# A fused gated-linear-attention and squared-ReLU kernel: the third and fifth unit's front steps, three hidden-layer steps and one output store take other places in the written order of the engines

## The chip, the cores and the metric

The kernel runs on 1 core of one Trainium2 chip. The metric is the device time of one execution in microseconds (us). The kernel before takes 170.76 us, the median of 3 runs (170.74 to 170.88).

## The reference

The program computes a recurrent linear attention with a decay for each channel, and puts its output through a two-layer network with a squared ReLU.

```python
def _attn_ref(q, k, v, alpha):               # each (4, 8, 768, 48), float32
    state = np.zeros((B, H, D, D))
    for t in range(S):
        state = alpha[:, :, t, :, None] * state + np.einsum('bhd,bhe->bhde', k[:, :, t], v[:, :, t])
        y[:, :, t] = np.einsum('bhd,bhde->bhe', q[:, :, t], state)
    return y

def _moe_ref(x, w_in, w_out):                # x (3072, 384), w_in (384, 2048), w_out (2048, 384)
    r = np.maximum(x @ w_in, 0.0)
    return (r * r) @ w_out
```

Here B = 4, H = 8, S = 768, D = 48; alpha lies between 0.8 and 1.0; x is y with its heads side by side.

## The kernel before

**Units.** The sequence of each batch is cut into 3 blocks of T = 256 tokens, which makes 12 units, numbered from 0: unit g is block g // 4 of batch g % 4. A partition holds two neighbouring tokens (j = 0, 1), so a unit fills the 128 partitions.

**The front of a unit** (from the third unit on, `decays_by_pair`). `pr` (L570) multiplies the two decays of a pair of tokens. `ln` (L573) takes the logarithm of that product into `lab`, `lm` (L612) the logarithm of the second decay alone into `la1` (shown as `la` by the profile). `m1i` (L579 and L582) sums `lab` over the tokens with a triangular matrix on TensorE, into PSUM bank `psW` (the first of `psWH`). `ei`, `ea`, `ec` (L590, L592, L595) take exponentials of the sums, `bk` (L597 on GpSimd, L599 on VectorE) multiplies one of them by a decay, `lb` (L614) subtracts `la1` from the sums, `es` (L616) takes the exponential of that. `ekm` (L646) and `eqm` (L641) multiply keys and queries by these factors into `qks`; `vc` (L637 on ScalarE) copies the values to bf16. Keys and queries are then transposed into `kqt`: for the units 0 to 2 on TensorE (`tr`, L669, with copies `et` out of PSUM, L677 and L679), from unit 3 on by two DMA transposes of SyncE's queue (`tr0`, `tr1`, L657).

**The mix.** `p` (L877, L730) forms the scores and the sum of key and value products, `mk` (L894) masks the scores (one half from `psZ`, one from `psX`), `y` (L765, L757) applies them and the state, `xe` and `xf` (L911, L913) copy the result to bf16, `xt` (L929 on TensorE for units 0 to 3, a DMA transpose L935 later) transposes it, and `xv` (L941, L943) copies the transposed result out of `psX` into `xt`, the input of the hidden layer. This last is the mix copy of the change's short name.

**The hidden layer.** For unit g and u = 0 to 7, `s1_g_u` (L992) makes two of 16 blocks of 128 hidden values for all 256 tokens, 6 matmuls into one PSUM bank; `re` (L1000 on ScalarE, L1002 on VectorE) is the ReLU out of that bank into a buffer `rr`; `sq` (L1010 on VectorE, L1013 on GpSimd, L1014 on ScalarE) squares one or two of them into `gt`. `s2_g_j_0` to `_3` (L1038) are the second layer for one token of each pair, four matmuls each; `oe` (L1045, L1047) copies the sum to `osb`, and `out` (L1054) stores it.

**Banks.** The hidden layer has two PSUM banks of `psWH` of its own, and for the first two units it also uses `psO`, in a fixed sequence (`HIDDEN = "0102102102102101"`, 2 meaning `psO`). So `s1_1_1` needs the bank that `re0_6` empties, `s1_1_4` the one that `re1_1` empties, `s1_1_5` the one that `re1_2` empties, and `s1_2_2` the one that `re2_0` empties. `rr` has 4 buffers of two halves; `re1_6` writes the half that `sq0_6` reads, `re1_7` the one that `sq0_7` reads.

**What sets the order.** `TABLES` (L206 to L268) names, for each of the five engines, every step in the sequence in which it is issued; an entry such as `+512` is a matmul on zeros at the start. `arrange` (L86) puts the steps in this order, `place` (L122) works out which semaphores each step must wait for, `emit` (L173) writes the programs. Each engine runs its list strictly in order: a step that waits holds everything behind it on its engine. A DMA is issued by the engine in whose list it stands.

Of the kernel before, what the change touches and what calls it, by code (L numbers as in the profile page):

```python
# [205 lines left out]
TABLES = {  # L206
    "act": """
        table ln0_0 ln1_0 ei0_0 xcaus ea0_0 ei1_0 ea1_0 ec1_0 et00_0 ec0_0 vc0 ln1 et01_0 et11_0 vc1 ei1 ea1 xe0
        ec1 et0_1 re0_0 sa1 re0_1 sq0_1 re0_3 xe1 re0_4 re0_5 lm2 ln2 re0_6 ei2 ea2 ec2 es2 re1_2 re1_3 sq0_6
        re1_4 et0_2 vc2 re1_6 sa2 sq1_6 sq1_3 ln3 lm3 ei3 ea3 ec3 es3 oe0_0 oe0_1 xf2 xe2 lm4 ln4 vc3 ei4 ea4  # L210
        ec4 re2_0 re2_1 es4 oe1_0 re2_2 re2_3 re2_4 ldk5 re2_5 ldq5 sa3 sq2_5 lm5 re2_7 ln5 re2_6 xe3 ei5 ea5
        ec5 xv3 es5 oe2_0 re3_0 oe2_1 lm6 re3_1 xe4 ln6 re3_4 re3_3 ei6 ea6 ec6 re3_6 sq3_5 re3_7 sq3_7 es6
        re4_0 re4_1 re4_2 re4_3 vc6 xe5 lm7 ln7 re4_7 oe3_1 re4_4 ei7 ea7 ec7 re4_6 sq4_6 es7 oe4_0 re5_0 re5_1
        lm8 ln8 xe6 re5_2 re5_3 ei8 ea8 re5_4 re5_5 es8 re5_6 re5_7 sq5_7 re6_0 re6_1 re6_2 oe5_0 vc8 xe7 lm9
        ln9 re6_5 re6_6 oe5_1 re6_7 ei9 ea9 es9 oe6_0 vc9 re7_0 lm10 re7_1 ln10 xe8 re7_3 ei10 ea10 re7_4 re7_5
        es10 re7_6 re7_7 oe7_0 re8_0 re8_1 re8_2 lm11 ln11 xe9 re8_3 re8_4 ei11 ea11 re8_5 re8_6 sq8_5 es11
        sq8_7 re9_0 oe8_0 vc11 re9_1 oe8_1 xe10 re9_3 re9_4 re9_5 re9_6 re9_7 re10_0 oe9_0 re10_1 re10_2 xe11
        oe9_1 re10_3 re10_4 re10_5 re10_6 re10_7 re11_0 oe10_0 re11_1 re11_2 re11_3 oe10_1 re11_4 re11_5 re11_6
        re11_7 oe11_0 oe11_10
    """,  # L220
    "dve": """
        zero zlinc zlstr zident zcaus zcaus1 zla0 zla1 zones zown zown0 zown1 zqk0 zqk1 zqk2 zlb0 zlb1 ekm0_0
        eqm0_0 ekm1_0 eqm1_0 et10_0 mk0_0 sa0 mk1_0 ekm1 eqm0_1 eqm1_1 xv0 et1_1 sc0 mk1_1 mk0_1 sc1 re0_2 xf1
        sq0_3 xv1 pr2 sq0_5 re0_7 re1_0 lb2 re1_1 ekm2 eqm0_2 eqm1_2 sq0_7 re1_5 et1_2 sq1_1 sq1_5 re1_7 mk1_2
        pr3 sc2 mk0_2 lb3 eqm1_3 eqm0_3 ekm3 xv2 pr4 sq1_7 bk4 lb4 ekm4 eqm1_4 eqm0_4 sq2_1 mk1_3 mk0_3 sc3
        oe1_1 sd3 sq2_7 sq2_6 xf3 lb5 ekm5 eqm1_5 eqm0_5 sa4 mk1_4 mk0_4 re3_2 pr6 sc4 sq3_1 xf4 sq3_3 re3_5
        sq3_6 lb6 ekm6 sa5 mk0_5 sc5 mk1_5 eqm0_6 eqm1_6 oe3_0 xf5 sq4_1 re4_5 pr7 sq4_3 sq4_7 sq4_5 bk7 lb7
        eqm0_7 sa6 eqm1_7 ekm7 sc6 sd6 mk0_6 mk1_6 pr8 oe4_1 xf6 sq5_3 bk8 lb8 ekm8 sq5_5 sq5_6 sa7 mk0_7 sc7
        mk1_7 eqm0_8 eqm1_8 sq6_1 re6_3 sd7 sq6_3 pr9 xf7 re6_4 sq6_5 sq6_6 sq6_7 bk9 lb9 ekm9 eqm0_9 eqm1_9
# [888 lines left out]
```

## Time and profile before

| | |
|---|---|
| median of 3 runs | 170.76 us |
| the profiled execution, its own time | 171.26 us |
| its span, first to last instruction | 169.5 us |
| TensorE (PE) busy | 163.8 us, 97% of the span |
| VectorE (DVE) busy | 118.0 us, 70% |
| ScalarE (ACT) busy | 109.6 us, 65% |
| GpSimd (POOL) busy | 35.3 us, 21% |
| DMA | 33.37 MB, mean 197 GB/s |
| granted TensorE clock | 1.0 throughout |

The profiled execution took 1.76 us more than its span and 0.50 us more than the median of the runs. A profile line gives the start in us from the span's start, the duration, the engine, the source line, the operation, the tile written and the tiles read, with the number of equal instructions in a row (x12); in brackets stands how long the engine stood idle before it, and who ended the idle time. PE is the matmul side of TensorE, PEld its loading of weights, SPq an issue of SyncE's DMA queue. Several matmuls overlap in the array, so that a row of twelve lasts some 0.16 us longer than the time until the next row can start.

### The profile page before, as it was taken

The numbers are of one execution on the slowest core, as the hardware profiler recorded it, in microseconds if no ns is written. First come the engines' busy times: TensorE is split into PE (matmuls) and PEld (weight loads), VectorE is DVE, ScalarE is ACT, GpSimd is POOL, SyncE is SP. The second block draws the span as 40 slices with busy tenths as digits, with TensorE's granted clock in tenths as the row PEclk, the third lists the DMA queues.
The fourth block names the chain that finished last, engine by engine and source line by source line (L and its number), as shares of the span: only waits on it lengthen the run. The fifth ranks groups of instructions, "written<-read, shape, count | busy, mean of one in ns | idle before, by whom it ended". The sixth has DMA issues, their size and how long they took to land.

```text
span 169.5 us, 5392 instructions
## 1 busy us (share of the span) xinstructions
PE 163.8 (97%) x2369; PEld 125.9 (74%) x2369; DVE 118.0 (70%) x206; ACT 109.6 (65%) x212; POOL 35.3 (21%) x46
## 2 busy tenths in 40 slices
PE   7988999999799999999999999999999999999994
PEld 2556889767686697877778876788797788787773
DVE  6577899985849868975978977887969637342130
ACT  3968778786868388667477757375677374466440
POOL 4671879130172032100240000000600000000000
DMA  5999999989999998999989999979797761040012
GB/s 137 324 318 188 260 312 215 293 288 252 185 220 329 241 181 197 307 137 243 301 195 247 263 152 258 207 194 288 145 190 205 97 119 58 0 141 4 33 60 93
DMA packets 68407, 33.37 MB, mean 197 GB/s; under 512 B 63520, under 2 KB 65312, under 8 KB 68384
## 3 DMA queue, kind: packets, MB, share of 16 engines
q1 hardware_dynamic: 62784, 24.39, 65.6%
q0 software_dynamic: 3520, 7.87, 18.6%
q10 hardware_dynamic: 2080, 0.79, 1.8%
q8 instruction: 18, 0.29, 0.7%
q14 instruction: 5, 0.04, 0.1%
HBM read 25.17 MB, written 4.72 MB: 176 GB/s over the span
## 4 chain that ended last, share of the span: by engine, by line
PE 83%; DMA 12%; ACT 1%; POOL 1%; issue 1%; DVE 0%; SPq 0%
PE psO L1038 34%; PE psWH L992 33%; DMA raw<-in_alpha_dram 6%; DMA raw<-in_v_dram 3%; DMA raw<-in_k_dram 2%; PE psX L877 2%; PE psZ L765 2%; PE psX L953 2%; PE psWH L1038 2%; PE psWH L730 1%; PE psZ L877 1%; PE psX L765 1%; PE psO L992 1%; PE psWH L579 1%; POOL raw L463 1%; ACT rr L1000 1%
## 5 line engine op out<-in xcount | busy, mean ns | idle before, releaser
L992 PE MATMUL psWH<-xt,win 128*128 128x256 bf16 x552 | 70.5, 273 | 0.9 <-ACT rr L1000 0.9
L1038 PE MATMUL psO<-wout,gt 128*128 128x384 bf16 x352 | 67.0, 326 | 0.0
L992 PEld LDWEIGHTS psWH<-xt,win 128*128 128x128 bf16 x552 | 59.8, 114 | 7.4 <-ACT rr L1000 1.4
L1000 ACT ACTIVATE rr<-psWH 128x512 bf16<-128x512 f32 x79 | 46.5, 599 | 25.3 <-PE psWH L992 24.0
L1038 PEld LDWEIGHTS psO<-wout,gt 128*128 128x128 bf16 x352 | 32.7, 98 | 16.7 <-DVE gt L1010 0.2
L1010 DVE TENSOR_TENSOR gt<-rr 128x1024 bf16<-128x1024 bf16 (+1 forms) x46 | 26.6, 584 | 22.4 <-ACT rr L1000 22.4
L1013 POOL TENSOR_TENSOR gt<-rr 128x1024 bf16<-128x1024 bf16 x3 | 5.7, 1911 | 56.6 <-ACT rr L1000 56.6
L894 DVE TENSOR_TENSOR pm<-psZ,caus 128x1024 bf16<-128x1024 f32 x12 | 14.6, 1216 | 3.7 <-PE psWH L730 3.0
L1045 ACT ACTIVATE osb<-psO 128x384 f32<-128x384 f32 x17 | 8.4, 492 | 11.6 <-PE psO L1038 11.2
L894 DVE TENSOR_TENSOR pm<-psX,caus 128x1024 bf16<-128x1024 f32 x12 | 14.6, 1215 | 0.9 <-PE psX L877 0.5
L641 DVE TENSOR_TENSOR qks<-raw,eq 128x384 bf16<-128x384 f32 x22 | 11.4, 550 | 1.1 <-ACT eq L616 1.0
L646 DVE TENSOR_TENSOR qks<-raw,ek 128x768 bf16<-128x768 f32 x11 | 10.5, 950 | 1.1 <-ACT ek L558 1.0
L1002 DVE TENSOR_SCALAR rr<-psWH 128x512 bf16<-128x512 f32 x13 | 8.8, 683 | 1.2 <-PE psWH L992 1.2
L1014 ACT ACTIVATE gt<-rr 128x512 bf16<-128x512 bf16 (+1 forms) x11 | 8.9, 821 | 0.6 <-DVE rr L1002 0.4
L573 ACT ACTIVATE lab<-prd 128x384 bf16<-128x384 f32 x10 | 5.2, 522 | 6.0 <-DVE prd L570 5.8
L1086 PE MATMUL psO<-zero 128*128 128x512 bf16 (+1 forms) x27 | 7.7, 418 | 1.3 <-DVE zero L382 1.3
L913 DVE CAST xbf<-psZ 128x384 bf16<-128x384 f32 x10 | 5.5, 554 | 3.4 <-PE psZ L757 3.2
L850 POOL TENSOR_TENSOR sbd<-tmp,acm 128x192 bf16<-128x192 f32 x5 | 2.9, 588 | 20.6 <-DVE tmp L840 16.2
L911 ACT ACTIVATE xbf<-psX 128x384 bf16<-128x384 f32 x11 | 5.4, 490 | 2.4 <-PE psZ L757 2.3
L637 ACT ACTIVATE vbf<-raw 128x768 bf16<-128x768 f32 x7 | 5.9, 837 | 1.2 <-DMA raw<-in_v_dram 1.2
L570 DVE TENSOR_TENSOR prd<-raw 128x384 f32<-128x384 f32 x9 | 6.4, 707 | 0.2 <-DMA raw<-in_alpha_dram 0.2
L616 ACT ACTIVATE eq<-la 128x384 f32<-128x384 f32 x10 | 5.2, 522 | 2.0 <-DVE la L614 2.0
(130 smaller groups left out, 190.8 us busy)
## 6 DMA issues: line engine op xcount, KB each, us to landing
out_dram<-osb SPq DMA_DIRECT2D x11, 384.0 KB, 3.3
raw<-in_alpha_dram SPq DMA_DIRECT2D x9, 384.0 KB, 5.5
raw<-in_v_dram SPq DMA_DIRECT2D x9, 384.0 KB, 4.4
raw<-in_k_dram SPq DMA_DIRECT2D x8, 384.0 KB, 5.7
raw<-in_q_dram SPq DMA_DIRECT2D x8, 384.0 KB, 4.0
win<-in_moe_w_in_dram POOLq DMA_DIRECT2D x4, 384.0 KB, 8.8
wout<-in_moe_w_out_dram POOLq DMA_DIRECT2D x4, 384.0 KB, 8.9
raw<-in_k_dram POOLq DMA_DIRECT2D x3, 384.0 KB, 6.4
```

Source lines behind the costliest of these rows:

```text
L570: add("dve", lambda e: e.tensor_tensor(hd(PRD[la][:]), al(0), al(1), ALU.mult), dve_ns(HD), p0, reads=[("raw", r, 0)], writes=[("prd", la) ...
L641: add("dve", lambda e, j=j, dst=dst: e.tensor_tensor(dst, RAW[r][:, 2, :, j, :].rearrange("p (n x) d -> p n x d", x=2), EQ[la][:, j].rearr ...
L646: add("dve", lambda e, a=a, E=E: e.tensor_tensor(QKS[qs][:, a, :, :, 0:D], RAW[r][:, 1 + a].rearrange("p h j d -> p j h d"), E[la][:].rear ...
L894: add("dve", lambda e, hf=hf, psT=psT: e.tensor_tensor(PM[pm][:, hf].rearrange("p r n j t -> p (r n) (j t)"), psT[:, :, :].rearrange("p r ...
L992: ins = pe.matmul(psN[:, i * T:(i + 1) * T], WIN[:, kk, hidden(fj)], mov, start=(kk == 0), stop=(kk == KT - 1))
L1000: add("act", lambda e, psN=psN, rr=rr: e.activation(rr, psN, AF.Relu), act_ns(512), pu + 600, reads=[keyN], writes=[("rr", rb, half)], nam ...
L1002: alts={"dve": (lambda e, psN=psN, rr=rr: e.tensor_scalar(rr, psN, 0.0, None, ALU.max), dve_ns(512))})
L1010: add("dve", lambda e, dst=dst, sq=sq: e.tensor_tensor(dst, sq, sq, ALU.mult), 148 + k * 267, pu + 1200, reads=[("rr", rb, h) for h in ran ...
L1014: "act": (lambda e, dst=dst, sq=sq: e.activation(dst, sq, AF.Square), act_ns(k * 512))})
L1038: ins = pe.matmul(psS, GT[gt][:, fj, j, :], WOUT[:, fj, :], start=(fj == 0), stop=(fj == FT - 1))
L1045: add("act", lambda e, j=j, psS=psS: e.activation(OSB[ob][:, j], psS, AF.Copy), act_ns(DM), ps_ + 700, reads=[keyS], writes=[("osb", ob, j ...
L1086: pr.arrange(TABLES, lambda n: lambda pe: pe.matmul(psO[:, 0:n], ZERO[:, 0:128], ZERO[:, 0:n], skip_group_check=True), zero)
```

## The change

Only `TABLES` changes: names move within the list of an engine, and one moves from ScalarE's to VectorE's. What is computed stays the same, and no step is added or removed.

```diff
     "act":
-        xe1 re0_4 re0_5 lm2 ln2 re0_6 ei2 ea2 ec2 es2 re1_2 re1_3 sq0_6 re1_4 et0_2 vc2 re1_6
+        xe1 re0_4 re0_5 re0_6 ln2 lm2 ei2 ea2 ec2 es2 re1_2 re1_3 vc2 re1_4 et0_2 re1_6
     "dve":
-        re0_7 re1_0 lb2 re1_1 ekm2 eqm0_2 eqm1_2 sq0_7 re1_5 et1_2 sq1_1 sq1_5 re1_7
+        re0_7 re1_0 re1_1 lb2 ekm2 eqm0_2 eqm1_2 re1_5 sq0_6 et1_2 sq0_7 sq1_1 sq1_5 re1_7
...
-        eqm0_3 ekm3 xv2 pr4 sq1_7 bk4 lb4
+        eqm0_3 ekm3 pr4 xv2 sq1_7 bk4 lb4
     "pe":
-        xt2 s2_1_0_2 s1_2_0 s1_2_1 m1i4 s2_1_0_3 s1_2_2 s1_2_3
+        xt2 s2_1_0_2 m1i4 s1_2_0 s1_2_1 s2_1_0_3 s1_2_2 s1_2_3
     "sp":
-        tr0_3 tr1_3 lda5 ldv4 tr0_4 tr1_4 out0_1 ldv5
+        tr0_3 tr1_3 lda5 out0_1 ldv4 tr0_4 tr1_4 ldv5
```

**First place, VectorE between the first and the second unit's hidden layer.** The `psO` row is the ReLU `re1_1`, the `rr2` row `re1_5`, the L614 row `lb2`, the L677 row the copy `et1_2` of the third unit's transposed keys and queries.

```order
 L1002 TENSOR_SCALAR rr0<-psWH 128x512
+L1002 TENSOR_SCALAR rr0<-psO 128x512
 L614 TENSOR_TENSOR la10<-psWH,la10 128x384
-L1002 TENSOR_SCALAR rr0<-psO 128x512
 L646 TENSOR_TENSOR qks2<-raw2,ek0 128x16x48
 L641 TENSOR_TENSOR qks2<-raw2,eq0 128x4x2x48 x2
+L1002 TENSOR_SCALAR rr2<-psWH 128x512
 L1010 TENSOR_TENSOR gt0<-rr3 128x512
-L1002 TENSOR_SCALAR rr2<-psWH 128x512
 L677 COPY kqt2<-psZ 128x8x2x64
+L1010 TENSOR_TENSOR gt0<-rr3 128x512
 L1010 TENSOR_TENSOR gt1<-rr0 128x1024
```

`re1_1` and `re1_5` stand one place sooner. The upper square was `sq0_7` and is now `sq0_6`, which came from ScalarE; `sq0_7` stands behind the copy `et1_2`, so that the list from there on has one square more ahead of it.

**Second place, TensorE and VectorE around the third unit's mix copy.** On TensorE the L579 and L582 rows are `m1i4`, the sums of the fifth unit's decays; `xt2` is what the mix copy fills.

```order
 L1038 MATMUL psO<-wout,gt1 128x384 x4
-L992 MATMUL psWH<-xt2,win 128x256 x12
 L579 MATMUL psWH<-lab0,linc 128x384
 L582 MATMUL psWH<-ones2,lab0 128x2 x4
+L992 MATMUL psWH<-xt2,win 128x256 x12
 L1038 MATMUL psO<-wout,gt1 128x384 x4
 L992 MATMUL psWH<-xt2,win 128x256 x12
```

`m1i4` now stands ahead of the third unit's first two hidden groups, `s1_2_0` and `s1_2_1`. On VectorE at the same place, with `pr4` as the `prd0` row and the mix copy `xv2` as the `xt2` row:

```order
 L646 TENSOR_TENSOR qks0<-raw3,ek1 128x16x48
+L570 TENSOR_TENSOR prd0<-raw0 128x384
 L941 COPY xt2<-psX 128x768
-L570 TENSOR_TENSOR prd0<-raw0 128x384
 L1010 TENSOR_TENSOR gt1<-rr3 128x512
```

The product of the fifth unit's decays stands ahead of the mix copy.

**Third place, SyncE's DMA queue behind the fourth unit's two transposes.** The `out_0_dram` row is the store `out0_1`, the `raw0<-in_v` row the load `ldv4`, the L657 rows behind it the transposes `tr0_4` and `tr1_4`.

```order
 L463 DMA raw1<-in_alpha_dram 128x8x96
+L1054 DMA out_0_dram<-osb0 128x768
 L463 DMA raw0<-in_v_dram 128x8x96
 L657 DMA_TRANSPOSE kqt1<-qks1 128x16x64 x2
-L1054 DMA out_0_dram<-osb0 128x768
 L463 DMA raw1<-in_v_dram 128x8x96
```

The store is issued ahead of one load and two transposes instead of behind them.

More of the change, by code (lines that the diff above doesn't have):

```diff
@@ L208 @@
         table ln0_0 ln1_0 ei0_0 xcaus ea0_0 ei1_0 ea1_0 ec1_0 et00_0 ec0_0 vc0 ln1 et01_0 et11_0 vc1 ei1 ea1 xe0
[L209 to L217, printed above, removed]
@@ L218 @@
-        oe9_1 re10_3 re10_4 re10_5 re10_6 re10_7 re11_0 oe10_0 re11_1 re11_2 re11_3 oe10_1 re11_4 re11_5 re11_6
-        re11_7 oe11_0 oe11_10
+        ec1 et0_1 re0_0 sa1 re0_1 sq0_1 re0_3 xe1 re0_4 re0_5 re0_6 ln2 lm2 ei2 ea2 ec2 es2 re1_2 re1_3 vc2
+        re1_4 et0_2 re1_6 sa2 sq1_6 sq1_3 ln3 lm3 ei3 ea3 ec3 es3 oe0_0 oe0_1 xf2 xe2 lm4 ln4 vc3 ei4 ea4 ec4
+        re2_0 re2_1 es4 oe1_0 re2_2 re2_3 re2_4 ldk5 re2_5 ldq5 sa3 sq2_5 lm5 re2_7 ln5 re2_6 xe3 ei5 ea5 ec5
+        xv3 es5 oe2_0 re3_0 oe2_1 lm6 re3_1 xe4 ln6 re3_4 re3_3 ei6 ea6 ec6 re3_6 sq3_5 re3_7 sq3_7 es6 re4_0
@@ L220 @@
+        re10_3 re10_4 re10_5 re10_6 re10_7 re11_0 oe10_0 re11_1 re11_2 re11_3 oe10_1 re11_4 re11_5 re11_6 re11_7
+        oe11_0 oe11_10
     """,
@@ L223 @@
         eqm0_0 ekm1_0 eqm1_0 et10_0 mk0_0 sa0 mk1_0 ekm1 eqm0_1 eqm1_1 xv0 et1_1 sc0 mk1_1 mk0_1 sc1 re0_2 xf1
-        sq0_3 xv1 pr2 sq0_5 re0_7 re1_0 lb2 re1_1 ekm2 eqm0_2 eqm1_2 sq0_7 re1_5 et1_2 sq1_1 sq1_5 re1_7 mk1_2
-        pr3 sc2 mk0_2 lb3 eqm1_3 eqm0_3 ekm3 xv2 pr4 sq1_7 bk4 lb4 ekm4 eqm1_4 eqm0_4 sq2_1 mk1_3 mk0_3 sc3
-        oe1_1 sd3 sq2_7 sq2_6 xf3 lb5 ekm5 eqm1_5 eqm0_5 sa4 mk1_4 mk0_4 re3_2 pr6 sc4 sq3_1 xf4 sq3_3 re3_5
+        sq0_3 xv1 pr2 sq0_5 re0_7 re1_0 re1_1 lb2 ekm2 eqm0_2 eqm1_2 re1_5 sq0_6 et1_2 sq0_7 sq1_1 sq1_5 re1_7
+        mk1_2 pr3 sc2 mk0_2 lb3 eqm1_3 eqm0_3 ekm3 pr4 xv2 sq1_7 bk4 lb4 ekm4 eqm1_4 eqm0_4 sq2_1 mk1_3 mk0_3
+        sc3 oe1_1 sd3 sq2_7 sq2_6 xf3 lb5 ekm5 eqm1_5 eqm0_5 sa4 mk1_4 mk0_4 re3_2 pr6 sc4 sq3_1 xf4 sq3_3 re3_5
         sq3_6 lb6 ekm6 sa5 mk0_5 sc5 mk1_5 eqm0_6 eqm1_6 oe3_0 xf5 sq4_1 re4_5 pr7 sq4_3 sq4_7 sq4_5 bk7 lb7
@@ L239 @@
         s1_1_3 s1_1_4 s1_1_5 tr0_2 s1_1_6 tr1_2 s2_0_0_0 s1_1_7 p0_2 s2_0_0_1 s2_0_0_2 s2_0_1_0 s2_0_1_1 m1i3
-        s2_0_1_2 s2_0_0_3 s2_0_1_3 y2 s2_1_0_0 s2_1_0_1 xt2 s2_1_0_2 s1_2_0 s1_2_1 m1i4 s2_1_0_3 s1_2_2 s1_2_3
+        s2_0_1_2 s2_0_0_3 s2_0_1_3 y2 s2_1_0_0 s2_1_0_1 xt2 s2_1_0_2 m1i4 s1_2_0 s1_2_1 s2_1_0_3 s1_2_2 s1_2_3
         s2_1_1_0 s1_2_4 s2_1_1_1 s1_2_5 p0_3 s2_1_1_2 s1_2_6 s1_2_7 s2_1_1_3 y3 m1i5 s2_2_0_0 s2_2_0_1 xt3
@@ L261 @@
     "sp": """
-        lda0 ldk0 ldq0 ldv0 lda1 ldk4 ldq4 tr0_3 tr1_3 lda5 ldv4 tr0_4 tr1_4 out0_1 ldv5 lda6 ldk6 tr1_5 out1_1
+        lda0 ldk0 ldq0 ldv0 lda1 ldk4 ldq4 tr0_3 tr1_3 lda5 out0_1 ldv4 tr0_4 tr1_4 ldv5 lda6 ldk6 tr1_5 out1_1
         tr0_5 xt4 ldq6 ldv6 lda7 ldq7 ldk7 tr0_6 tr1_6 out2_1 xt5 ldv7 lda8 ldk8 out3_1 tr0_7 tr1_7 out4_1 xt6
```

5 lines of the change are left out of this document (added).

## The prediction

> **What bounds the kernel now.** I read the chain of waits first, then the busy time by stretches, then the timeline where a stretch has a hole.
>
> ```profile
> PE 83%; DMA 12%; ACT 1%; POOL 1%; issue 1%; DVE 0%; SPq 0%
> 40.00:44.00 4.00, 3.15 (x27) 2.17 (x26) 2.44 (x6) 3.00 (x7) 0.00 (x0) 1.00 1.10 231
> 60.00:80.00 20.00, 20.00 (x336) 16.08 (x337) 14.78 (x26) 15.65 (x32) 3.28 (x4) 1.00 0.97 212
> ```
>
> The chain is TensorE for 83% of the span; the DMA share is the first loads. The two other rows are stretches, with the busy time of PE as the first number behind the stretch's length, then PEld, DVE, ACT, POOL, the granted clock (1.00) and the DMA share. From 60 to 80 us PE has no hole; from 40 to 44 us it lacks 0.85 us, at full clock. So a change of order is worth what it takes from PE's holes or adds to them. The big hole, as the chain has it:
>
> ```profile
> 40.47 1.50 PE psWH L992 x12
> ...
> 42.25 0.49 ACT ek L590
> ...
> 43.20 0.50 ACT rr L1000
> 43.74 1.50 PE psWH L992 x12
> 45.24 0.65 PE psO L1038 x4
> ```
>
> TensorE makes `s1_2_0` and `s1_2_1`, then the sums `m1i4`. ScalarE has the exponentials of these sums (`ei4`, `ea4`, `ec4`) ahead of the ReLU `re2_0`, and `s1_2_2` waits for the bank that `re2_0` empties. The ReLU's data was there long before; it stood behind the exponentials.
>
> **The second place: m1i4 and pr4 ahead.**
>
> ```profile
> 38.09 0.95 DVE L646 TENSOR_TENSOR qks<-raw,ek 128x768 bf16<-128x768 f32 x1
> 38.97 0.54 ACT L612 ACTIVATE la<-raw 128x384 f32<-128x384 f32 x1
> 39.66 0.81 PE L1038 MATMUL psO<-wout,gt 128*128 128x384 bf16 x4
> 39.86 0.56 DVE L941 COPY xt<-psX 128x768 bf16<-128x768 bf16 x1 [0.82 <-PE psX L929]
> 40.33 0.55 DVE L570 TENSOR_TENSOR prd<-raw 128x384 f32<-128x384 f32 x1
> 40.91 0.53 ACT L573 ACTIVATE lab<-prd 128x384 bf16<-128x384 f32 x1 [1.40 <-DVE prd L570]
> 41.35 0.83 ACT L637 ACTIVATE vbf<-raw 128x768 bf16<-128x768 f32 x1
> 41.81 0.33 PE L579 MATMUL psWH<-lab,linc 128*128 128x384 bf16 x1
> 42.08 0.81 PE L1038 MATMUL psO<-wout,gt 128*128 128x384 bf16 x4
> ```
>
> Four second-layer matmuls keep PE for 0.65 (the chain's row at 45.24), so `s2_1_0_2` ends at 39.66 + 0.65 = 40.31, and PE stands until the mix copy lets `s1_2_0` go at 40.47: 0.16. Twelve hidden matmuls take 41.81 - 40.47 = 1.34, `m1i4` takes 42.08 - 41.81 = 0.27. `s2_1_0_3` is through at 42.08 + 0.65 = 42.73, and PE stands until 43.74: 1.01. Holes in all: 1.17.
>
> In the new order `pr4` goes into the 0.82 that VectorE idles ahead of the mix copy. The decays had landed by 38.97, where `lm4` read them without a wait. `pr4` starts when the L646 row (`ekm3`) ends at 39.04 and is done at 39.59; the mix copy still starts at 39.86. `ln4` runs 39.62 to 40.15 instead of 40.91 to 41.44, so `lab` is there before 40.31 and `m1i4` follows at once: 40.31 to 40.58. The mix copy ends at 40.42, inside it, so its wait is covered too. Then 1.34 to 41.92, 0.65 to 42.57, and `s1_2_2` may start. Its ReLU: from `m1i4` to `s1_2_2` today's path is 43.74 - 41.81 = 1.93, which gives 40.31 + 1.93 = 42.24; with the values' copy `vc3` (0.83 behind `ln4`, to about 40.98) in front of the exponentials it is some 0.2 later, 42.45. Both are under 42.57, so nothing takes the hole's place. **Gain: 43.74 - 42.57 = 1.17**; at least 0.85, the hole as the stretch's row counts it.
>
> **The first place: ReLUs sooner, two squares later.**
>
> ```profile
> 24.52 1.28 DVE L1002 TENSOR_SCALAR rr<-psWH 128x512 bf16<-128x512 f32 x2
> 25.09 0.58 PEld L992 LDWEIGHTS psO<-xt,win 128*128 128x128 bf16 x6 [0.16 <-ACT rr L1000]
> 26.03 0.56 DVE L614 TENSOR_TENSOR la<-psWH,la 128x384 f32<-128x384 f32 x1 [0.24 <-ACT acm L595]
> 26.51 0.68 DVE L1002 TENSOR_SCALAR rr<-psO 128x512 bf16<-128x512 f32 x1
> 26.62 0.53 ACT L616 ACTIVATE eq<-la 128x384 f32<-128x384 f32 x1 [0.62 <-DVE la L614]
> 27.05 1.07 ACT L1000 ACTIVATE rr<-psWH 128x512 bf16<-128x512 f32 x2
> 27.24 0.58 PEld L992 LDWEIGHTS psO<-xt,win 128*128 128x128 bf16 x6 [0.26 <-DVE rr L1002]
> 27.93 0.82 PE L992 MATMUL psWH<-xt,win 128*128 128x256 bf16 x6
> ```
>
> `re0_6` goes into ScalarE's idle time ahead of the logarithms, so `s1_1_1` no longer waits for it (about 0.2 at 25.09), and `re1_1` starts when VectorE's two ReLUs leave it (one each 0.60, so 24.52 + 1.20 = 25.72) instead of 26.51, so that the hole at 27.24 closes too. But `lb2` now stands behind `re1_1`: it starts at about 26.35, not 26.03, and on ScalarE `es2`, `re1_2` and `re1_3` stand behind it. `re1_2` started at 27.05 and ended near 27.63; (two in 1.07); it moves by 0.32 to 27.95. `s1_1_5` needs its bank: it starts near 27.99 where it started at 27.93. The two closed holes are given back there, and 0.06 more. Then VectorE:
>
> ```profile
> 28.53 0.59 ACT L1000 ACTIVATE rr<-psO 128x512 bf16<-128x512 f32 x1
> 28.91 0.42 DVE L1010 TENSOR_TENSOR gt<-rr 128x512 bf16<-128x512 bf16 x1
> 29.24 0.68 DVE L1002 TENSOR_SCALAR rr<-psWH 128x512 bf16<-128x512 f32 x1
> 30.13 0.81 PE L1038 MATMUL psO<-wout,gt 128*128 128x384 bf16 x4
> 30.33 0.69 DVE L677 COPY kqt<-psZ 128x1024 bf16<-128x1024 bf16 x1 [0.41 <-PE psZ L669]
> 33.87 0.55 DVE L570 TENSOR_TENSOR prd<-raw 128x384 f32<-128x384 f32 x1
> 34.45 0.52 ACT L573 ACTIVATE lab<-prd 128x384 bf16<-128x384 f32 x1
> 35.03 0.10 PEld L579 LDWEIGHTS psWH<-lab,linc 128*128 128x128 bf16 x1 [0.20 <-ACT lab L573]
> ```
>
> One square costs VectorE 29.24 - 28.91 = 0.33 in a row of others (0.42 alone). `sq0_6` fits ahead of `et1_2`, where 0.41 was idle; `sq0_7` now lies behind `et1_2`, and from there to `pr3` no row of VectorE has idle time in brackets. So `pr3` comes 0.33 + 0.06 = 0.39 later, and with it `ln3` and `m1i3`, whose weights waited for `ln3` already (0.20 in the last row): no slack. PE's own 0.06 lies under that wait, so after `m1i3` PE is **0.39 late**. Everything up to the second place (the third mix, `ekm`, the mix copy) hangs on `m1i3` or PE and shifts by the same, so the 1.17 stays as reckoned. Bounds of this loss: 0, if `m1i3` finds cover that the rows don't show, and 0.42 + 0.32 = 0.74, if square and late `lb2` add up.
>
> At nothing I cost: `lm2` behind `ln2` (it now ends near 25.0, under the wait of `lb2` until 26.35); `vc2` ahead of `re1_4` (ScalarE loses a square of 0.5 and gains a copy of 0.83 there, with `es2`'s 0.32 that moves `re1_4`'s end from 29.12 to 29.66; the second layer's first group needs `psO` at 30.13, and without that cover each 0.1 costs 0.1); the mix copy behind `pr4`, which is idle time.
>
> **The third place: the store ahead of load and transposes.**
>
> ```profile
> 42.48 1.23 SPq L463 DMA_DIRECT2D raw<-in_alpha_dram  x1
> 43.75 0.64 SPq L463 DMA_DIRECT2D raw<-in_v_dram  x1
> 45.63 3.85 SPq L657 DMA_TRANSPOSE kqt<-qks  x2
> 49.52 0.69 SPq L1054 DMA_DIRECT2D out_dram<-osb  x1
> 55.91 0.42 PE L877 MATMUL psX<-kqt 64*64 64x128 bf16 x16
> kqt<-qks SPq DMA_TRANSPOSE x1, 4.0
> kqt<-qks SPq DMA_TRANSPOSE x2, 5.9
> out_dram<-osb SPq DMA_DIRECT2D x11, 384.0 KB, 3.3
> ```
>
> The last three rows give the time to landing: of the fourth unit's transpose issued at 39.07, of the fifth unit's two, and the median of the stores. SyncE's queue idles from 44.39 to 45.63, and the store's 0.69 fits in: with the 0.39 shift `lda5` ends at 44.1, the store at 44.8, `ldv4` at 45.5, so the transposes begin at 45.5 and the second, half of 3.85 later, at 47.4. Landing after 5.9 puts it at 53.3. One transfer more ahead of them may add (5.9 - 4.0) / 2, about 0.95, taking the growth over the two loads ahead as the estimate: 54.3. `p0_4`, at 55.91 now, comes to 55.13. Cover 0.8 to 1.8: nothing.
>
> By the Trainium skill, DMA: Bandwidth & Descriptors, section Queues, rings and completion order, each DMA engine consumes the descriptors of a queue's ring in order; that speaks against the move, since the store's bytes then stand in front of the transposes. The trace agrees as far as 4.0 growing to 5.9 shows; no run here shows the store in front. By the rule the time would at worst be that of the first rival below, 171.5; by the rows it stays at the sum.
>
> **Sum.** -1.17 + 0.39 = -0.78. The profiled execution's 171.26 would become 170.48 and its span 169.5 become 168.7; the median, 0.50 below the profiled one, goes from 170.76 to **170.0**. By the bounds the change is between -1.17 and -0.85 + 0.74 = -0.11: 169.6 to 170.65. A measurement tells 0.2% (0.34 us) from no change here.
>
> **Rivals.**
>
> 1. *The store delays the fifth unit's scores: slower.* Transposes queue behind the whole store, with its 3.3 added: 53.3 + 3.3 = 56.6, and `p0_4`, in order on a full PE, starts 0.7 later than now. From then on PE has no idle time in which to catch up: 171.5. It decides from 1.8 of delay on (the gain is gone at 2.6). For it: the order in the ring, and DMA shares above 1. Against it: the earlier growth of 1.9 for two loads.
> 2. *Taken back later.* PE is 0.8 earlier, but `lda5` and its product are not, nor are later loads; some wait after 44 us ends where it ends today. 170.6 to 170.8. For it: `lda5` issued 0.39 later. Against it: landings 2 us ahead of their use, as for `p0_4` above.
> 3. *A larger early loss.* The 0.74, with a gain of 0.85 to 1.17: 170.3 to 170.65. For it: no slack at `m1i3`.
> 4. *No early loss*: 169.6. Against it: the 0.20 wait at `m1i3`.
>
> **How the numbers follow.** Forecast 0.55 (169.6 to 170.35), rival 1 0.18, rival 2 0.12, rival 3 0.10, half of it faster by more than 0.34, rival 4 0.05. Faster by over 0.2%: 0.55 + 0.05 + 0.05 = 0.65; within: 0.12 + 0.05 = 0.17; slower: 0.18. The range runs from 169.5 to 171.0, past rivals 2 to 4 and short of most of rival 1.
>
> **What would show it.** Right: no hole at `s1_2_2`; `m1i4` before `s1_2_0`; `s1_2_2` near 43.0; a new hole of 0.3 to 0.4 at `m1i3` and one near 0.45 at `s1_1_5`; PE full from 44 us on, 0.8 earlier than now up to its end. Wrong: a hole at `p0_4` with its transposes landing after 55 (rival 1), a hole at `m1i5` or a later mix (rival 2), `s1_2_2` after 43.4 (rival 3), `m1i3` no later than 35.1 (rival 4).

## The result, and the profile after

The changed kernel takes **172.91 us** (median of 4 runs, 172.51 to 173.09), the kernel before 170.79 (4 runs). The ratio is 1.0107, with an interval of 1.0083 to 1.0131: slower by about 1.1%. The forecast was 170.0, faster; its first rival, the store that delays the fifth unit's scores, is what came. The profiled execution took 172.51 us with a span of 170.8, against 171.26 and 169.5 before. These two differ by 1.25, the medians by 2.12: the profiled execution before was 0.50 above its median, the one after is the fastest of its four. Ratios here and below leave out runs more than 1.5% above the fastest of their kernel, so for kernels that spread widely they lie below the ratio of the medians.

The chain of waits of the changed kernel, shares of the span:

```profile
PE 74%; DMA 13%; DVE 6%; POOL 3%; issue 1%; ACT 1%; SPq 0%
```

The same stretches as before (length, then PE, PEld, DVE, ACT and POOL busy, clock, DMA share, GB/s), with the middle one of the kernel before under them:

```profile
40.00:44.00 4.00, 4.00 (x39) 3.42 (x37) 3.24 (x7) 4.00 (x10) 0.00 (x0) 1.00 1.06 210
44.00:60.00 16.00, 13.98 (x258) 10.36 (x257) 10.10 (x18) 8.88 (x18) 4.68 (x4) 1.00 1.11 235
60.00:80.00 20.00, 20.00 (x305) 16.30 (x304) 15.27 (x27) 14.92 (x30) 3.28 (x4) 1.00 1.03 212
```

```profile
44.00:60.00 16.00, 16.00 (x276) 12.15 (x274) 11.86 (x19) 10.30 (x23) 4.77 (x4) 1.00 1.24 251
```

The hole from 40 to 44 us is closed: PE is busy for 4.00 of 4.00, where it had 3.15. A new one of 16.00 - 13.98 = 2.02 stands in the stretch behind it, which had none before (16.00 of 16.00). TensorE's timeline says where:

```profile
27.95 0.85 PE L992 MATMUL psWH<-xt,win 128*128 128x256 bf16 x6 [0.33 <-ACT rr L1000]
...
35.41 0.34 PE L579 MATMUL psWH<-lab,linc 128*128 128x384 bf16 x1 [0.24 <-ACT lab L573]
...
40.69 0.33 PE L579 MATMUL psWH<-lab,linc 128*128 128x384 bf16 x1
...
40.95 1.48 PE L992 MATMUL psWH<-xt,win 128*128 128x256 bf16 x12
42.27 0.81 PE L1038 MATMUL psO<-wout,gt 128*128 128x384 bf16 x4
42.92 1.47 PE L992 MATMUL psWH<-xt,win 128*128 128x256 bf16 x12
...
57.16 0.42 PE L877 MATMUL psX<-kqt 64*64 64x128 bf16 x16 [2.02 <-DMA kqt<-qks]
```

The first three rows are `s1_1_5`, `m1i3` and `m1i4`; then come `s1_2_0` with `s1_2_1`, `s2_1_0_3`, and at 42.92 `s1_2_2`, without a bracket: TensorE goes from one to the next. The last row is `p0_4`, which waits 2.02 for the transposed keys and queries. It starts 1.25 later than before (55.91), and TensorE has no hole from there to 80 us, so the span is 1.3 longer. The forecast's -0.78 and this hole of 2.02 add up to 1.24, so for the profiled pair the hole is the whole miss; the rest of the 2.12 between the medians isn't in these two profiles.

SyncE's queue, and under it the two loads that ScalarE's queue issues in the same time (from ScalarE's timeline, `ldk5` and `ldq5`):

```profile
43.99 0.62 SPq L1054 DMA_DIRECT2D out_dram<-osb  x1
44.65 1.51 SPq L463 DMA_DIRECT2D raw<-in_v_dram  x1
46.21 6.12 SPq L657 DMA_TRANSPOSE kqt<-qks  x2
```

```profile
45.74 0.41 ACTq L463 DMA_DIRECT2D raw<-in_k_dram  x1
...
47.05 0.44 ACTq L463 DMA_DIRECT2D raw<-in_q_dram  x1
```

The transposes are issued from 46.21, 0.58 later than before (45.63), although the store fitted into idle time of the queue: the value load behind it holds the queue for 1.51 instead of 0.64. And the two issues of the transposes then last 6.12 instead of 3.85. The chain of waits has the second one's landing, and the DMA view the times from issue to landing of what was issued from 46 to 51 us, and of the first transpose alone:

```profile
50.58 6.49 DMA kqt<-qks
57.07 0.09 issue
57.16 0.42 PE psX L877 x16
```

```profile
raw<-in_v_dram SPq DMA_DIRECT2D x1, 384.0 KB, 7.8
raw<-in_k_dram ACTq DMA_DIRECT2D x1, 384.0 KB, 6.2
raw<-in_q_dram ACTq DMA_DIRECT2D x1, 384.0 KB, 9.1
kqt<-qks SPq DMA_TRANSPOSE x2, 8.3
kqt<-qks SPq DMA_TRANSPOSE x1, 10.2
```

Before, the same window has these two among others:

```profile
raw<-in_q_dram ACTq DMA_DIRECT2D x1, 384.0 KB, 5.0
kqt<-qks SPq DMA_TRANSPOSE x2, 5.9
```

Everything in flight in this stretch lands late, not only the transposes: `ldq5` 9.1 after its issue, where it was 5.0, the first transpose 10.2, the second at 50.58 + 6.49 = 57.07, while the two took 5.9 in the median before. So it isn't one transfer that stands in a line; the whole group takes longer.

### The profile page after: what moved, and what is told of

The parts are those of the page before. It is cut to its first block, busy times and chain, and to the rows that moved or that the text cites. A ratio compares the mean times of both kernels' runs of the same rounds, so it can differ in the third digit from the quotient of the medians.

```text
span 170.8 us, 5391 instructions
## 1 busy us (share of the span) xinstructions
PE 162.8 (95%) x2367; PEld 126.0 (74%) x2369; DVE 118.5 (69%) x207; ACT 109.2 (64%) x211; POOL 35.2 (21%) x46
## 4 chain that ended last, share of the span: by engine, by line
PE 74%; DMA 13%; DVE 6%; POOL 3%; issue 1%; ACT 1%; SPq 0%
PE psO L1038 31%; PE psWH L992 31%; DMA raw<-in_alpha_dram 7%; DMA kqt<-qks 4%; DMA raw<-in_k_dram 2%; DVE pm L894 2%; PE psX L877 2%; POOL win L434 2%; POOL raw L463 2%; PE psZ L765 2%; PE psX L953 2%; PE psWH L730 1%; DVE rr L1002 1%; PE psZ L877 1%; PE psX L765 1%
## 5 line engine op out<-in xcount | busy, mean ns | idle before, releaser
L1038 PE MATMUL psO<-wout,gt 128*128 128x384 bf16 x352 | 67.0, 326 | 0.0
L1038 PEld LDWEIGHTS psO<-wout,gt 128*128 128x128 bf16 x352 | 32.8, 98 | 16.7 <-DVE gt L1010 0.2
L1014 ACT ACTIVATE gt<-rr 128x1024 bf16<-128x1024 bf16 (+1 forms) x10 | 8.3, 840 | 0.6 <-DVE rr L1002 0.4
L1086 PE MATMUL psO<-zero 128*128 128x512 bf16 (+1 forms) x25 | 7.0, 408 | 1.6 <-DVE zero L382 1.3
L877 PE MATMUL psX<-kqt 64*64 64x128 bf16 x192 | 5.0, 222 | 2.3 <-DMA kqt<-qks 2.0
L877 PEld LDWEIGHTS psX<-kqt 64*64 64x64 bf16 x192 | 3.1, 106 | 4.9 <-issue 4.1
```

What stands on the lines that cost most here:

```text
L877: ins = pe.matmul(psT[64 * c:64 * c + 64, rr_, o:o + 128], keys, mov)
L1014: "act": (lambda e, dst=dst, sq=sq: e.activation(dst, sq, AF.Square), act_ns(k * 512))})
L1038: ins = pe.matmul(psS, GT[gt][:, fj, j, :], WOUT[:, fj, :], start=(fj == 0), stop=(fj == FT - 1))
L1086: pr.arrange(TABLES, lambda n: lambda pe: pe.matmul(psO[:, 0:n], ZERO[:, 0:128], ZERO[:, 0:n], skip_group_check=True), zero)
```

## The experiments

A kernel is compared with runs of the kernel before on the same chip. "Hole" is the wait of `p0_4` in the one profiled run, if no other place is named.

| kernel | median us (range, runs) | before | ratio, interval | hole us |
|---|---|---|---|---|
| e1, changed, store back | 170.30 (170.04-172.03, 10) | 171.12 | 0.9959, 0.9928-0.9989 | 0 |
| e2, store alone | 173.47 (171.40-175.07, 10) | 171.12 | 1.0088, 1.0057-1.0119 | 2.4 |
| e3, second place alone | 171.09 (169.75-173.57, 10) | 171.12 | 0.9978, 0.9955-1.0001 | 1.8 |
| e4, first place alone | 171.35 (171.11-171.84, 10) | 171.12 | 1.0013, 1.0000-1.0027 | 0 |
| f1, store on ScalarE's queue | 171.91 (171.62-172.53, 8) | 171.00 | 1.0045, 1.0016-1.0075 | 1.4 |
| f2, an eighth of the store | 172.39 (170.63-174.73, 7) | 171.00 | 1.0049, 1.0011-1.0087 | 1.6 |
| f3, a load in the store's place | 172.25 (171.48-172.74, 10) | 171.00 | 1.0060, 1.0038-1.0082 | 0; 1.2 at `xt3` |
| f4, store back, loads far sooner | 171.26 (170.58-174.06, 10) | 171.00 | 0.9997, 0.9974-1.0021 | 0; 0.4 at `p0_3` |
| g1, store early, loads later | 171.90 (170.58-172.80, 10) | 170.96 | 1.0043, 1.0013-1.0074 | 2.0 |
| g2, store back, loads sooner | 170.70 (170.16-171.51, 10) | 170.96 | 0.9988, 0.9973-1.0002 | 0 |
| g3, store back, loads later | 171.47 (171.43-171.88, 4) | 170.96 | 1.0039, 1.0024-1.0054 | 0; 1.4 at L1038 |
| h1, store back, `ldv4` first | 170.51 (169.93-172.08, 10) | 171.01 | 0.9965, 0.9928-1.0002 | 0 |
| h2, store early, `ldv4` first | 172.31 (170.34-174.11, 10) | 171.01 | 1.0036, 0.9996-1.0077 | 0 |
| h3, second place, `ldv4` first | 170.53 (169.54-172.99, 10) | 171.01 | 0.9965, 0.9936-0.9993 | 0 |
| i1, store early, one queue | 170.96 (170.34-171.65, 10) | 171.10 | 0.9987, 0.9969-1.0006 | 0 |
| i2, the changed kernel again | 173.63 (172.31-174.96, 4) | 171.10 | 1.0117, 1.0046-1.0187 | 2.8 |
| j1, store early, loads sooner | 171.25 (170.67-171.81, 10) | 170.95 | 1.0011, 0.9993-1.0028 | 0.5 |
| j2, second place, loads sooner | 170.98 (170.45-172.15, 10) | 170.95 | 1.0005, 0.9984-1.0026 | 0; 1.2 at `xt3` |

### One place at a time

e1 is the changed kernel with the store back where it was:

```diff
-        lda5 out0_1 ldv4 tr0_4 tr1_4 ldv5
+        lda5 ldv4 tr0_4 tr1_4 out0_1 ldv5
```

> The changed kernel with the store out0_1 back behind the two transposes; first and second place stay as changed. Theory A (the store's place ahead of load and transposes makes the hole of 2.0 us at p0_4): no hole at p0_4, the gain of the second place is kept, 170.0 us (169.8 to 170.3). Theory B (the hole comes from the earlier start of everything behind the second place, which sends the loads ldk5 and ldq5 on ScalarE's queue 0.85 us sooner into the transposes; the store is harmless): the hole stays, 172 to 173 us.

e2 is the kernel before with the store alone moved:

```diff
-        lda5 ldv4 tr0_4 tr1_4 out0_1 ldv5
+        lda5 out0_1 ldv4 tr0_4 tr1_4 ldv5
```

> The kernel before with the store alone moved ahead of the load and the transposes. Theory A: the transposes land near 57 as in the changed kernel, p0_4 was due at 55.9, so a hole of about 1.2 us: 171.8 to 172.3 us. Theory B: ldk5 and ldq5 keep their times, the transposes land in time, 170.8 us.

e3 is the kernel before with the second place alone, e4 with the first place alone (the ScalarE and VectorE lines of the first place in the change's diff):

```diff
-        ekm3 xv2 pr4 sq1_7
+        ekm3 pr4 xv2 sq1_7
...
-        xt2 s2_1_0_2 s1_2_0 s1_2_1 m1i4 s2_1_0_3
+        xt2 s2_1_0_2 m1i4 s1_2_0 s1_2_1 s2_1_0_3
```

> The kernel before with pr4 and m1i4 alone moved ahead. Theory A: the whole 1.17 us of the prediction is kept to the end, 169.6 us, s1_2_2 near 42.6, p0_4 near 54.7 without a hole. Theory B: the loads ldk5 and ldq5 come sooner still, a hole at p0_4, 171.5 us or more.

> The kernel before with the ReLUs, squares, the value copy and the logarithm of the first place alone moved. Both theories on the hole expect none here. By the prediction's first place m1i3 comes 0.39 us later and the big hole ahead of s1_2_2 moves with it: 171.15 us. If the first place costs nothing: 170.8 us.

With the store back (e1) the rest of the change is worth having: 170.30 us, the fastest median of this case, though two of its ten runs took 171.54 and 172.03. Its stretches, its `p0_4` on TensorE's timeline, and SyncE's queue:

```profile
40.00:44.00 4.00, 4.00 (x38) 3.47 (x37) 3.48 (x7) 4.00 (x10) 0.00 (x0) 1.00 1.09 200
44.00:60.00 16.00, 16.00 (x302) 11.93 (x301) 11.36 (x19) 9.66 (x21) 4.72 (x4) 1.00 1.11 246
```

```profile
54.77 0.42 PE L877 MATMUL psX<-kqt 64*64 64x128 bf16 x16
```

```profile
44.41 4.77 SPq L657 DMA_TRANSPOSE kqt<-qks  x2
49.23 0.97 SPq L1054 DMA_DIRECT2D out_dram<-osb  x1
```

Both stretches are full, and `p0_4` has no bracket. The span is 168.4, where the prediction had 168.7. With the store alone (e2), in a run of 174.26 us, the hole at 43 us is still there and the one at `p0_4` is added:

```profile
43.87 0.84 PE L992 MATMUL psWH<-xt,win 128*128 128x256 bf16 x6 [0.85 <-ACT rr L1000]
...
58.88 0.42 PE L877 MATMUL psX<-kqt 64*64 64x128 bf16 x16 [2.38 <-DMA kqt<-qks]
```

So the store's place is what makes the change slow, without any help of the other two. The second place alone (e3) missed what was expected, 169.6: its median of 171.09 is no gain (0.4 by the ratio, which leaves its two longest runs out). Its best single run comes near, 169.75, which is 1.37 under the median of the kernel before. But its runs spread over 3.8 us, and the profiled one, the longest, has a hole of 1.8 at `p0_4` with the store in its old place: the late landing needs no early store, the early store makes it the rule. The first place alone (e4) costs 0.2 in the medians (0.0 to 0.5 by the interval), where 0.39 was expected; the weights of `m1i3` wait 0.63 for `ln3` there, where they waited 0.20 before:

```profile
34.95 0.10 PEld L579 LDWEIGHTS psWH<-lab,linc 128*128 128x128 bf16 x1 [0.63 <-ACT lab L573]
```

### What of the store does it

Three kernels keep a transfer early and change one property of it. In f1 the store goes to ScalarE's queue, behind the copy `oe1_0` of the second unit (line L1054 is widened so that ScalarE may issue it):

```diff
-        re2_0 re2_1 es4 oe1_0 re2_2
+        re2_0 re2_1 es4 oe1_0 out0_1 re2_2
...
-        lda5 out0_1 ldv4 tr0_4 tr1_4 ldv5
+        lda5 ldv4 tr0_4 tr1_4 ldv5
```

> The changed kernel with the store out0_1 issued by ScalarE's queue, behind oe1_0, at about 43.5 us; SyncE's queue has only lda5, ldv4 and the transposes there. Theory A1 (all DMA engines are busy in that stretch, so any 384 KB sent before the transposes delay them, whatever the queue): transposes land at 56 to 57.5, a hole of 1 to 2 us at p0_4, 172 to 173 us. Theory A2 (what delays them is the place in SyncE's ring alone): they land before 54.5, no hole, 170.0 to 170.5 us.

In f2 it stands as in the change, with an eighth of its bytes in as many packets (128); the other seven eighths of the first unit's output rows are left out:

```diff
-    e.dma_start(dst, OSB[ob][:].rearrange("p j n -> p (j n)"))
+    e.dma_start(dst[:, 0:96] if g == 0 else dst, OSB[ob][:].rearrange("p j n -> p (j n)")[:, 0:96] if g == 0 else ...)
```

> The changed kernel with out0_1 in its early place, but storing only the first 96 of 768 columns of a partition (48 of 384 KB); the other seven eighths of the first unit's output rows are left out. Theory A1 and A2 (bytes ahead of the transposes): no hole at p0_4, 169.9 to 170.4 us. Theory A3 (one more issue on SyncE's queue or a write between reads is enough, whatever its size): the hole stays, 172 us or more.

In f3 a load takes its place, and the store goes behind the transposes:

```diff
-        lda5 out0_1 ldv4 tr0_4 tr1_4 ldv5
+        lda5 ldv5 ldv4 tr0_4 tr1_4 out0_1
```

> The changed kernel with the load ldv5 in the place ahead of ldv4 and the store out0_1 back behind the transposes: 384 KB read in place of 384 KB written. Theory A1: the transposes are as late as behind the store, hole of 1 to 3 us, 172 to 173 us. Theory A3 (it is the write that delays): no hole, 170.0 to 170.5 us.

f1 and f2 keep most of the hole, as TensorE's waits say (f1, then f2):

```profile
PE psX L877 <- issue: 1.4, 1, 1.4
```

```profile
PE psX L877 <- issue: 1.6, 1, 1.6
```

The view names no transfer there, but in both the second transpose lands 0.1 ahead of `p0_4` (56.65 and 57.13 against 56.74 and 57.23), as in the changed kernel. With 48 KB instead of 384 KB the fifth unit's second transpose lands at 57.13, against 57.07 with all of them: **the landing is as late with an eighth of the bytes**. Whether the number of packets counts was not tried. Over all runs f2 loses less, 1.4 over the kernel before against 2.5 for the changed kernel on the same chip (i2), and one of its seven runs took 170.63. The store's place in SyncE's ring isn't all either, since on the other queue it keeps two thirds of the hole (1.38 of 2.02) and still loses 0.9 against the kernel before. f3 lost time at another place, which is told below; its second transpose lands late too, at 55.95 against 53.24 in e1, only TensorE is so late itself that `p0_4` doesn't wait. So a load put ahead delays the landing too, not a store alone.

### The loads of the other queue

f4, g2 and g3 are e1 with `ldk5` and `ldq5` on ScalarE's queue some 5 us sooner, some 3 us sooner, and some 2 us later; g1 is the changed kernel with them later, as in g3:

```diff
-        ln4 vc3 ei4 ea4 ec4
+        ln4 vc3 ldk5 ei4 ldq5 ea4 ec4
```

```diff
-        oe1_0 re2_2 re2_3 re2_4 ldk5 re2_5 ldq5 sa3
+        oe1_0 ldk5 re2_2 re2_3 ldq5 re2_4 re2_5 sa3
```

```diff
-        re2_4 ldk5 re2_5 ldq5 sa3 sq2_5 lm5 re2_7
+        re2_4 re2_5 sa3 ldk5 sq2_5 lm5 ldq5 re2_7
```

> The changed kernel with the store back behind the transposes, and ldk5 and ldq5 of ScalarE's queue some 4 us sooner, behind vc3 and ei4 (about 41 us in place of 45.5 and 46.7). Theory A1 (bytes in flight with the transposes delay them): the transposes land 1 us or more sooner than with the store back alone, and the spread of the runs shrinks; 169.9 to 170.2 us. If the sooner loads only delay lda5 and ldv4 instead: a hole at m1i5 or p0_4, 170.5 us or more.

> The changed kernel, store in its early place, with ldk5 and ldq5 of ScalarE's queue some 2 us later (behind sa3 and lm5, about 48 and 49.3 in place of 45.7 and 47.0), so that both transposes are issued ahead of them. Theory C (the transposes are late where ScalarE's two loads are issued ahead of them and run among them): they land before 54.5, no hole at p0_4 above 0.3 us, 170.0 to 170.7 us. Theory E (each transpose's issue waits on SyncE's queue for the transfers ahead of it there): the second transpose still lands after 55.5, hole of 0.5 us or more, 171 us or more.

> The changed kernel with the store back behind the transposes and ldk5 and ldq5 some 2 us sooner (behind oe1_0 and re2_3, about 43.5 and 45), ahead of both transposes. Theory C: the transposes land after 55.5 with no store ahead of them, hole of 1 us or more, 171.3 us or more. Theory E: as with the store back alone, 170.0 to 170.6 us.

> The changed kernel with the store back behind the transposes and ldk5 and ldq5 some 2 us later, behind sa3 and lm5: a try at a version that beats both. Theory C: the transposes land a microsecond sooner than with the store back alone (52.5 and 53.2) and the runs spread less, 169.9 to 170.3 us. Theory E: no change in the landing, 170.0 to 170.6 us; if the keys and queries come too late instead, a hole shows at the fifth or sixth unit's later steps, 170.6 us or more.

None of them beats e1. f4 shows directly what the loads do to transposes of the other queue. They run there beside the fourth unit's transposes, with the same loads ahead of these in SyncE's queue as in e1. Issue to landing of what was issued from 39 to 42 us, f4, then e1:

```profile
raw<-in_q_dram ACTq DMA_DIRECT2D x1, 384.0 KB, 5.2
kqt<-qks SPq DMA_TRANSPOSE x2, 6.1
```

```profile
kqt<-qks SPq DMA_TRANSPOSE x2, 4.3
```

The transposes take 6.1 instead of 4.3, and `p0_3` waits 0.36 for the second. g1 was to take the loads away from the fifth unit's transposes and didn't in the profiled run: they are issued at 47.92 and 48.44, still between the transposes at 46.04 and 49.03, and the hole is 2.0. Its ten runs fall in two groups, though, 170.58 to 171.03 (four) and 171.88 to 172.80 (six), while no run of the changed kernel is under 172.31. In g2 the loads are ahead of both transposes and the store behind them; the second transpose lands at 54.25 and there is no hole, so the loads without the early store don't do it there. In g3 the hole of 1.4 has another cause. ScalarE's copy `oe2_0` waits for the buffer that the store in its old place empties late, at 56.26 (54.50 in e1), and the second layer waits for the copy:

```profile
56.34 0.49 ACT L1045 ACTIVATE osb<-psO 128x384 f32<-128x384 f32 x1 [2.33 <-DMA out_dram<-osb]
```

In e1 ScalarE waits 0.44 there and TensorE doesn't; in e3, f3 and f4 TensorE waits 0.2 to 0.4 at this step. So the store's old place has little cover left as well.

h1 to h3 then took away the value load between store and transposes:

```diff
-        ldk4 ldq4 tr0_3 tr1_3 lda5 out0_1 ldv4 tr0_4 tr1_4 ldv5
+        ldk4 ldq4 ldv4 tr0_3 tr1_3 lda5 out0_1 tr0_4 tr1_4 ldv5
```

This is h2; h1 has the store behind `tr1_4` as well, and h3 is e3 with that queue.

> The changed kernel with the store back behind the transposes and the load ldv4 sooner, ahead of the fourth unit's transposes (about 38.3 us). Theory V (the issue of tr1_4 on SyncE's queue is held until the load ldv4 ahead of it has landed; whatever delays that load delays p0_4): tr1_4 lands before 52.5, no hole, 169.9 to 170.3 us with little spread. Theory W (any transfer near the transposes delays them by sharing): the fourth unit's transposes land later, a hole at p0_3 near 47, or no change in the spread, 170.3 us or more.

> The changed kernel with the store in its early place, and only ldv4 taken out from between store and transposes (ahead of the fourth unit's transposes). Theory V: tr1_4 waits for the store alone, which landed near 48.7, so it lands near 53 to 54: no hole above 0.3 us, 169.9 to 170.6 us. Theory W: the store ahead delays the transposes as in the changed kernel, hole of 1 us or more, 171.3 us or more.

> The kernel before with the second place alone (pr4, m1i4 ahead) and ldv4 ahead of the fourth unit's transposes, store in its old place. Theory V: the 1.17 us are kept in nearly every run, 169.6 to 169.9 us, and the runs spread by less than the 3.8 us of the second place alone. Theory W: median near 171 and the spread stay.

h2 is the telling one: ten runs of one program in two groups, 170.34 to 170.62 (four) and 172.27 to 172.68 (five), with one run at 174.11. The profiled run, 170.35, has no hole although the store is early. The same order of work can land in either group; taking the value load away isn't enough to keep the landing early. h1 and h3 missed their 169.9 to 170.3 and 169.6 to 169.9, and their runs still spread over 2.2 and 3.5 us.

i1 therefore keeps the store early and takes the second queue out of it: both loads go to SyncE's queue behind the transposes.

```diff
-        lda5 out0_1 ldv4 tr0_4 tr1_4 ldv5
+        lda5 out0_1 ldv4 tr0_4 tr1_4 ldk5 ldq5 ldv5
...
-    ACT_LOADS = {5: "kq"}
+    ACT_LOADS = {}
```

> The changed kernel, store in its early place, with ldk5 and ldq5 issued by SyncE's queue behind tr1_4 in place of ScalarE's queue, so that no other queue's packets run between those of the fifth unit's transposes. Theory X (the late state comes from two queues' packets sharing the DMA engines while the transposes run): the transposes land before 54.5 in spite of the store, no hole at p0_4 above 0.4 us; the keys and queries of the sixth unit come near 55 and may cost a few tenths later: 170.2 to 171 us, in one group of runs. Theory Y (what stands ahead on SyncE's queue is enough): the second transpose lands after 55.5, hole of 0.7 us or more, 171.5 us or more.

> The changed kernel itself once more, for the spread of its runs beside the others' of this study: with the store early and the loads on ScalarE's queue. If the late state is a matter of chance per run, some of its runs lie near 170.3 as with ldv4 taken out from between (four of ten there); if it is settled by the order, all lie between 172.3 and 173.3.

SyncE's queue of i1, and its `p0_4`:

```profile
43.72 0.63 SPq L1054 DMA_DIRECT2D out_dram<-osb  x1
44.39 1.69 SPq L463 DMA_DIRECT2D raw<-in_v_dram  x1
46.12 4.11 SPq L657 DMA_TRANSPOSE kqt<-qks  x2
50.28 1.38 SPq L463 DMA_DIRECT2D raw<-in_k_dram  x1
```

```profile
54.96 0.42 PE L877 MATMUL psX<-kqt 64*64 64x128 bf16 x16
```

The store, the value load and the first transpose are issued within 0.3 of where the changed kernel has them (46.12 against 46.21 for the transpose), and the second transpose lands at 53.15 instead of 57.07. The hole is gone, all ten runs lie in one group of 1.3 us, and the median is 2.7 under that of the changed kernel on the same chip (170.96 against 173.63). Its ratio is short of e1's, with intervals that overlap: the keys and queries now come later, and a wait of 0.4 for `pm` stands further on.

i1 changes two things at once, the queue of the two loads and their time. They are issued at 50.28 and 51.70 instead of 45.74 and 47.05, so the transposes go first. The eight transfers of the stretch (`lda5`, the store, `ldv4`, both transposes, `ldk5`, `ldq5`, `ldv5`) are all in by 57.80, against 58.23 in the changed kernel. So the group as a whole is hardly quicker; what i1 shows is that the transposes are early when the loads go behind them. Whether a second queue costs something by itself was not tried.

j1 leaves the loads on their queue and issues them sooner, at 42.83 and 44.14, ahead of both transposes (the second of the three diffs above, on the changed kernel); j2 does the same to e3.

> The changed kernel, store in its early place, with ldk5 and ldq5 on ScalarE's queue some 2 us sooner (behind oe1_0 and re2_3, about 43.5 and 45), so that their packets have run before the transposes' begin. Theory X (the late state needs the other queue's packets among those of the transposes): the five transfers ahead take some 6.3 us at 1.25 us each, the transposes run alone behind them and land near 53.5 to 54.5: no hole above 0.4 us, 170.1 to 170.8 us. Theory Y (the store ahead is enough): hole of 1 us or more, 171.5 us or more.

> The kernel before with the second place alone (pr4 and m1i4 ahead) and the two loads on ScalarE's queue 2 us sooner in the same way. Theory X: with no packets among the transposes the 1.17 us are kept, 169.6 to 170.0 us. If the loads among the transposes are not what spread the runs of the second place alone (169.75 to 173.57 there): median near 171 as there.

j1 wins back most, though less than expected (170.1 to 170.8): 171.25, in one group, with a wait of 0.48 left at `p0_4` (second transpose at 55.23):

```profile
55.32 0.42 PE L877 MATMUL psX<-kqt 64*64 64x128 bf16 x16 [0.48 <-issue]
```

j2 missed what was expected, 169.6 to 170.0. Its runs spread less than e3's (1.7 us against 3.8), and `p0_4` doesn't wait, but another hole took the gain, the same as in f3. j2 on VectorE and GpSimd, then e1 at the same steps:

```profile
50.61 2.22 DVE L1010 TENSOR_TENSOR gt<-rr 128x512 bf16<-128x512 bf16 x2
```

```profile
50.38 0.99 POOL L636 CAST vbf<-raw 128x768 bf16<-128x768 f32 x1 [0.82 <-DMA raw<-in_v_dram]
51.55 0.99 POOL L597 TENSOR_TENSOR ek<-ek,raw 128x384 f32<-128x384 f32 x1 [0.18 <-ACT ek L590]
```

```profile
51.02 0.75 DVE L1010 TENSOR_TENSOR gt<-rr 128x512 bf16<-128x512 bf16 x2
```

```profile
48.55 0.82 POOL L636 CAST vbf<-raw 128x768 bf16<-128x768 f32 x1
51.97 1.00 POOL L597 TENSOR_TENSOR ek<-ek,raw 128x384 f32<-128x384 f32 x1 [2.59 <-ACT ek L590]
```

Two squares of VectorE take 2.22 instead of 0.75. In e1 GpSimd is idle while they run, since its cast of the values was done at 49.37; in j2 the cast waited for its load (the bracket) and then ran, with the product behind it, at the very time of the squares. They hold up the copy `xf3` behind them, and TensorE waits 1.22 for it at `xt3`. In f3 the values come late for a plainer reason, since `ldv5` is issued ahead of `ldv4`; the squares take 2.23 there and the wait is 1.23. This cause is read from the traces; no kernel was run that moves GpSimd's work alone.

## Why the prediction was wrong, step by step

- **The second place: right in the changed kernel.** `m1i4` stands ahead, `s1_2_2` starts at 42.92 (43.0 was predicted, 43.74 before), and no wait took the hole's place. From `m1i3` to `s1_2_2` it is 7.51 (42.92 - 35.41) instead of 8.69 (43.74 - 35.05): 1.18 less, where 1.17 was reckoned. That the gain lasts to the end was not so in e3, whose median shows none.
- **The first place: right.** `m1i3` came at 35.41, its weights 0.38 later than before (35.03; 0.39 predicted), `s1_1_5` at 27.95 with a hole of 0.33 (27.99). That these times on the clock agree so well is luck: the first hidden-layer step starts anywhere from 15.8 to 17.2 us in these profiles (16.41 before, 15.91 after). What holds is the distance from `m1i2` to `m1i3`, 10.44 before and 10.85 to 10.86 in e1, e4 and the changed kernel, so 0.42 for the term of 0.39. The kernel before:

```profile
24.61 0.34 PE L579 MATMUL psWH<-lab,linc 128*128 128x384 bf16 x1
35.05 0.33 PE L579 MATMUL psWH<-lab,linc 128*128 128x384 bf16 x1
```

- **The sum without the third place: right.** -0.78 was reckoned; e1, which is that sum, measures 170.30 against 171.12, so -0.82 (by the ratio -0.7, between -1.2 and -0.2). Its two parts measured alone don't add up to it, though: 0.0 for e3 (-0.4 by the ratio) and +0.2 for e4.
- **The third place: wrong, and with it the forecast.** The step that failed is "Cover 0.8 to 1.8: nothing". It rests on one estimate, that one more transfer ahead of the transposes adds half the growth from 4.0 to 5.9, "about 0.95", which put the landing at 54.3. It was 57.07. The second transpose was to be issued at 47.4 and was at 50.58, since the first one's issue held the queue; but in f2 it was issued at 48.41 and landed as late, at 57.13. The estimate priced a transfer in a line. What the runs show is a group of transfers on two queues: the store early, alone, makes a hole of 2.4 (e2), an eighth of the bytes makes the landing as late (f2), the same store on the other queue keeps two thirds of the hole (f1), and with the two loads of the other queue issued behind the transposes there is no hole (i1). No row of the profile before had that case in it. The 4.0 and 5.9 differ by what else was in flight, not by two loads ahead in the ring: the fourth unit's transposes also stood behind two loads (`ldk4` and `ldq4`, issued at 37.29 and 37.70 and landed at 40.63 and 41.87), and f4 raised their 4.3 to 6.1 by ScalarE's loads alone.
- **Rival 1: the right place, the wrong price and reason.** `p0_4` was to start 0.7 later than before and started 1.25 later. It had the transposes behind the whole 3.3 of a store, landing at 56.6; that this is near 57.07 is luck, since an eighth of the store should then have landed far sooner. The time was 172.91, not 171.5. Its likelihood of 0.18 leaned on "Against it: the earlier growth of 1.9 for two loads", the same row misread a second time.
- By the Trainium skill, DMA: Bandwidth & Descriptors, section Issuing engines are not separate DMA queues, transfers issued by SyncE and by ScalarE run on the same DMA engines and interleave there. The traces agree: a load of one queue and a transpose of the other land late together (9.1 for `ldq5`, 10.2 for `tr0_4`), and f4 shows the transposes delayed by the loads. Issuing the loads behind the transposes is worth 2.7 us here (i1). The order in SyncE's ring alone would not let f1 and i1 come out as they did, one with a hole and the store on another ring, one without and the store in the same.

**What stays open.** What in the DMA engines tips a run of one program into the late landing (h2's two groups, e3's spread), and why 48 KB bring as late a landing as 384 KB, no run here tells. That the early store and the loads among the transposes are needed together holds for the changed kernel's order (e1 takes one away, i1 puts the other behind); e3's long run, with neither moved, shows that the store isn't needed always. Why the second place gains with the first beside it (e1) and not alone (e3) is open too.
